# Moving the last output-weight load behind the last V blocks, and giving the wait for the output to GpSimd

## The chip, the cores and the metric

One core of a Trainium2 chip. The metric is the device time of one execution in microseconds, median of several runs. "The trace" is the hardware profile of one of those executions; its span (first to last instruction) is about 1.8 us less than the device time.

## The reference

One decode step of grouped-query attention over a long cache, mixed by a gate with a small MLP. Only the attention matters here:

```python
def _A_ref(x, k_cache, v_cache, wq, wo):         # x [1,1,448], caches [1,8,65536,256] bf16
    q = (x @ wq).reshape(1, 1, 16, 256)...       # 16 query heads, 8 key/value heads, 2 queries share one
    scores = jnp.einsum("bhqd,bhkd->bhqk", q, k) * (256 ** -0.5)
    p = _softmax(scores, axis=-1)
    o = jnp.einsum("bhqk,bhkd->bhqd", p, v)
    return o.transpose(...).reshape(1, 1, 16 * 256) @ wo      # wo [4096, 448]
...
return g * a + (1 - g) * b                       # a: attention, b: MLP, g: gate
```

The two caches are 537 MB. Everything else is small.

## The kernel before

The sequence is cut into 48 chunks (8 key/value heads, 6 chunks each, 5 or 6 times 2048 positions). All large loads are issued by SyncE, in one order that is also the order of the DMA queue. K has two buffers, V one; a load waits until its buffer is free (`s_vf`). The output weights of a head group (512 rows of `wo`, 448 KB) have one buffer, and are loaded once for each group behind the group's second V chunk:

```python
        load_k(2)
        for i in range(1, total - 1):
            load_v(i)
            if i % PER == 1 and i > PER:       # PER = 6 chunks for each head group
                load_wo(i // PER)              # waits for s_oo: the group before has used its weights
            if i + 2 < total:
                load_k(i + 2)
        ...
        vlast = kbuf[(total - 2) % 2]          # the last V chunk goes to a free K buffer, in four pieces
        edges = [0, nlast - TURN - SB, nlast - TURN, nlast - TAIL, nlast]    # rows 0, 40, 56, 76, 80
        for k in range(len(edges) - 1):
            lo, hi = edges[k] * DH, edges[k + 1] * DH
            sp.dma_start(out=vlast[:, lo:hi], in_=src[:, lo:hi]).then_inc(s_last[k], 16)
```

At the end, the last 24 rows of V are used as stationary operand ("turned"), so that the head's output comes out as a column; then the output weights are applied and the row is stored:

```python
        pe.wait_ge(s_last[2], 16)
        turned(edges[2], edges[3])             # 40 matmuls
        pe.wait_ge(s_last[3], 16)
        turned(edges[3], edges[4]).then_inc(s_fp, 1)     # 8 matmuls
        take(dve, s_wo, 16)
        dve.wait_ge(s_fp, 4)
        heads().then_inc(s_fd, 1)              # VectorE: oT = PSUM * gate / denominator
        pe.wait_ge(s_fd, 4)
        for k in range(4):
            cc, r = divmod(k, 2)               # r: which of the two heads
            for a in range(4):
                ins = pe.matmul(acc4[32 * a:32 * a + 1, 0:DQ], lhsT=oT[:, k:k + 1],
                                rhs=wo[:, r, cc, DQ * a:DQ * (a + 1)], ...)
        ins.then_inc(s_fp, 1)
        dve.wait_ge(s_fp, 5)
        dve.tensor_copy(out=res[0:97, :], in_=acc4[0:97, 0:DQ]).then_inc(s_fd, 1)
        sp.wait_ge(s_fd, 5)
        sp.dma_start(out=out[0, 0]..., in_=res[0:97:32, :]).then_inc(s_out, 16)
        sp.wait_ge(s_out, 16)
```

After this the language adds an end: SyncE signals all engines, each drains and answers, SyncE collects the answers, and a barrier in two rounds follows.

The softmax here doesn't subtract the row's maximum and nothing guards it: scores larger than these inputs give would overflow.

## Time and profile before

| | before |
|---|---|
| device time, median of 3 | 1268.15 us (1268.02 to 1268.16) |
| span of the profiled run | 1266.2 us |
| DMA, share of 16 engines' span | 99.5%, 544 MB at 430 GB/s |
| PE, VectorE busy | 57%, 53% |

The page's second part (busy tenths in 40 slices) and its third (queue, packets, MB, share of 16 engines) show a kernel with nothing left but bytes:

```profile
DMA  9999999999999999999999999999999999999997
...
q1 hardware_dynamic: 16728, 544.22, 99.5%
```

So only the two ends of the span can shrink. The chain of waits, in order of time (start, length, what; all in us), ends so:

```profile
1229.60 0.04 issue
1229.64 31.00 DMA kbuf<-in_A_v_cache_dram
1260.64 0.05 issue
1260.69 1.44 PE misc L798 x48
1262.13 0.02 issue
1262.15 0.17 DVE oT L569
1262.33 0.04 issue
1262.37 0.57 PE acc L831 x14
1262.94 0.02 issue
1262.96 0.27 DVE res L838
```

The 31 us are the time a V piece spends in the queue, not the time it takes. What counts is 1260.64: the landing that lets PE start the 48 turned matmuls. The chain stops at `res`; the rest is read from SyncE's waits (who waited for whom: us in total, times, longest):

```profile
SPq L841 <- DVE res L838: 32.7, 1, 32.7
...
SPq L846 <- DMA out_dram<-res: 1.0, 1, 1.0
```

The trace has the store issued at 1263.27, its last semaphore step at 1264.92, and 1.29 us more to the end of the span.

### The profile page before, as it was taken

Reading aid. Unit: us, or ns where it says so; the run is one execution under the profiler, and the core shown is the slowest. Engines: PE = TensorE matmul, PEld = TensorE weight load, DVE = VectorE, ACT = ScalarE, POOL = GpSimd, SP = SyncE. Lnnn points to the kernel's source line nnn. Section 1 sums busy time; section 2 is a strip of 40 time slices with the busy share of each in tenths; the row PEclk is TensorE's granted clock in tenths of the full one; section 3 lists DMA queues with packets and bytes.
Section 4 is the critical chain, followed back from the end, with each engine's and each line's share of the span. In section 5 each row is a group of like instructions: output and inputs, shape, how many; then the busy total and the mean of one; then the engine's idle time right before and its main releaser. Section 6 shows DMA issues by size and latency. Waiting matters only on the chain. (4 is left out here: it accounts for less than half of the span.)

```text
span 1266.2 us, 10795 instructions
## 1 busy us (share of the span) xinstructions
PE 719.7 (57%) x4344; PEld 281.9 (22%) x4344; DVE 665.2 (53%) x473; ACT 50.1 (4%) x127; POOL 76.8 (6%) x98
## 2 busy tenths in 40 slices
PE   2845656566554665456555664565545655467646
PEld 1311222122221222122222221222212222122212
DVE  4745554465544645455445554565445644465444
ACT  0000000000000000000000000000000000000000
POOL 0001010110101101101111011000000000000000
PEclk9887877778777778778877788778867778777787
DMA  9999999999999999999999999999999999999997
GB/s 409 420 442 435 427 439 435 425 435 443 424 437 434 433 438 434 430 429 432 436 439 434 429 435 438 425 438 434 435 433 436 430 430 435 437 436 434 429 432 323
DMA packets 16828, 544.35 MB, mean 430 GB/s; under 512 B 1840, under 2 KB 3890, under 8 KB 4146
## 3 DMA queue, kind: packets, MB, share of 16 engines
q1 hardware_dynamic: 16728, 544.22, 99.5%
q8 instruction: 4, 0.07, 0.0%
q14 instruction: 6, 0.05, 0.0%
q10 hardware_dynamic: 90, 0.01, 0.0%
HBM read 544.22 MB, written 0.00 MB: 430 GB/s over the span
## 5 line engine op out<-in xcount | busy, mean ns | idle before, releaser
L677 PE MATMUL sc<-kT,qw 128*128 128x512 bf16 x2048 | 562.7, 437 | 455.9 <-PEq L673 455.9
L551 DVE STREAM_TRANSPOSE kT<-kbuf 128x2048 f32<-128x2048 f32 x256 | 571.1, 2283 | 309.6 <-DVEq L543 309.6
L677 PEld LDWEIGHTS sc<-kT,qw 128*128 128x128 bf16 x2048 | 213.5, 108 | 804.1 <-issue 639.6
L691 PE MATMUL pv<-vbuf,pT 128*4 128x512 bf16 x2008 | 132.4, 417 | 56.7 <-PEq L725 56.7
L597 DVE STREAM_TRANSPOSE pT<-p_t 128x512 bf16<-128x512 bf16 x48 | 34.1, 711 | 116.9 <-DVEq L543 116.9
L562 DVE TENSOR_TENSOR og<-pv,og 128x512 f32<-128x512 f32 x39 | 27.0, 691 | 111.1 <-DVEq L543 108.5
L691 PEld LDWEIGHTS pv<-vbuf,pT 128*4 128x4 bf16 x2008 | 51.4, 93 | 136.0 <-issue 98.1
L624 ACT ACTIVATE p_t<-sc 128x512 bf16<-128x512 f32 x48 | 28.7, 597 | 1191.8 <-PE sc L677 1191.8
L651 POOL TENSOR_SCALAR t_b<-t_b 128x448 f32<-128x448 f32 x14 | 7.9, 564 | 358.2 <-ACT t_b L633 358.2
L655 POOL TENSOR_SCALAR t_b<-t_b,hw 128x448 f32<-128x448 f32 x14 | 8.9, 638 | 335.4 <-ACT t_b L641 335.4
L561 DVE COPY og<-pv 128x512 f32<-128x512 f32 x8 | 5.5, 691 | 38.9 <-DVEq L543 38.9
L660 POOL TENSOR_TENSOR ymix<-ymix,t_b 128x448 f32<-128x448 f32 x14 | 16.1, 1148 | 1.1
L747 PE MATMUL acc<-wo,oT 128*1 128x448 bf16 x28 | 8.7, 445 | 12.7 <-PEq L744 12.7
L654 POOL TENSOR_TENSOR t_b<-t_b,u_b 128x448 f32<-128x448 f32 x14 | 15.8, 1127 | 1.2
L659 POOL TENSOR_TENSOR t_b<-t_b,u_b 128x448 f32<-128x448 f32 x14 | 15.8, 1126 | 1.2
L633 ACT ACTIVATE t_b<-h_bc,b1T,w1T 128x448 f32<-128x448 f32 x14 | 10.5, 748 | 0.0
L647 POOL TENSOR_SCALAR u_b<-h_bc,w1T,b1T 128x448 f32<-128x448 f32 x14 | 10.0, 714 | 4.1 <-DVE pat L426 2.7
L624 ACT ACTIVATION_READ_ACCUMULATOR p_t<-sc 128x1 f32 x48 | 9.3, 194 | 0.0
L701 PEld LDWEIGHTS misc<-mask,og 128*128 128x128 f32 x64 | 8.7, 196 | 2.3 <-DVE og L562 1.3
L701 PE MATMUL misc<-mask,og 128*128 128x2 f32 (+1 forms) x64 | 8.0, 249 | 0.8 <-DVE og L562 0.8
L641 ACT ACTIVATE t_b<-t_b 128x448 f32<-128x448 f32 x14 | 7.9, 566 | 0.0
L747 PEld LDWEIGHTS acc<-wo,oT 128*1 128x1 bf16 x28 | 2.2, 91 | 15.4 <-issue 14.5
(98 smaller groups left out, 55.6 us busy)
## 6 DMA issues: line engine op xcount, KB each, us to landing
kbuf<-in_A_k_cache_dram SPq DMA_DIRECT2D x32, 5120.0 KB, 33.2
vbuf<-in_A_v_cache_dram SPq DMA_DIRECT2D x31, 5120.0 KB, 20.8
kbuf<-in_A_k_cache_dram SPq DMA_DIRECT2D x16, 6144.0 KB, 36.0
vbuf<-in_A_v_cache_dram SPq DMA_DIRECT2D x16, 6144.0 KB, 24.7
wo<-in_A_wo_dram SPq DMA_DIRECT2D x8, 448.0 KB, 22.1
vbuf<-in_A_wq_dram SPq DMA_DIRECT2D x1, 3072.0 KB, 10.2
kbuf<-in_A_v_cache_dram SPq DMA_DIRECT2D x1, 2560.0 KB, 26.5
kbuf<-in_A_v_cache_dram SPq DMA_DIRECT2D x1, 1280.0 KB, 31.0
```

Of the source, the lines that this page charges most:

```text
L551: dve.transpose(out=kT[b][:].bitcast(FP32), in_=kn[:, s * SB * 128:(s + 1) * SB * 128]).then_inc(s_kt, 1)
L562: return dve.tensor_tensor(out=og[:], in0=pv[:], in1=og[:], op=ALU.add)
L597: dve.transpose(out=pT[:], in_=p_t[:]).then_inc(s_pt, 1)
L624: ins = act.activation(out=p_t[:], in_=sc[:], func=ACT.Exp, scale=scale, accum_out=den[:, c:c + 1])
L633: ins = act.activation(out=t_b[:], in_=h_bc[:], func=ACT.Square, scale=w1T[:, b:b + 1], bias=b1T[:, b:b + 1],)
L654: lambda: pool.tensor_tensor(out=t_b[:], in0=t_b[:], in1=u_b[:], op=ALU.mult),
L659: lambda: pool.tensor_tensor(out=t_b[:], in0=t_b[:], in1=u_b[:], op=ALU.mult),
L660: lambda: pool.tensor_tensor(out=ymix[:], in0=ymix[:], in1=t_b[:], op=ALU.add),
L677: ins = pe.matmul(sc[:], lhsT=qw[:, q, at:at + 128], rhs=kv[:, :, q // 2, :, q % 2], start=(first and q == 0), stop=(last and q == 7), ski ...
L691: ins = pe.matmul(pv[32 * a:32 * a + 4, :], lhsT=pT[:, k, :, ROW0 + s], rhs=vt[:, j * DH:(j + 2) * DH], start=first and k < 4, stop=last a ...
L701: ins = pe.matmul(o_ps[:, cc, 0:width if half == 0 else 2], lhsT=og[:, half * DH + cc:(half + 1) * DH:2], rhs=mask[:, m:m + (width if half ...
L747: ins = pe.matmul(acc[0:1, 0:D], lhsT=oT[:, k:k + 1], rhs=wo[:, r, cc, :], start=False, stop=False, skip_group_check=True,)
```

## The change

The last group's weights are not needed before the very last matmuls. The intent is to let them use the time in which PE and VectorE work on the last V rows, and to bring V forward by the time the weights took in front of it. The second head's weights get their own semaphore, and the loop is turned so that the first head's matmuls come first. The final wait moves to GpSimd, so that SyncE can start the closing exchange while the store is in flight.

```diff
-            if i % PER == 1 and i > PER:
+            if i % PER == 1 and PER < i < total - PER:
                 load_wo(i // PER)
@@ behind the four last V pieces
+        sp.wait_ge(s_oo, HKV - 1)
+        s_wl = [nc.alloc_semaphore(f"s_wl{r}") for r in range(2)]
+        for r in range(2):
+            at = (HKV - 1) * 512 + r * DH
+            sp.dma_start(
+                out=wo[:, r, :, :].rearrange("p c n -> p (c n)"),
+                in_=A_wo[at:at + DH, :].rearrange("(p c) n -> p (c n)", c=2),
+            ).then_inc(s_wl[r], 16)
@@ at the end
-        take(dve, s_wo, 16)
...
-            cc, r = divmod(k, 2)
+            r, cc = divmod(k, 2)
+            if cc == 0:
+                pe.wait_ge(s_wl[r], 16)
...
-                    acc4[32 * a:32 * a + 1, 0:DQ], lhsT=oT[:, k:k + 1],
+                    acc4[32 * a:32 * a + 1, 0:DQ], lhsT=oT[:, 2 * cc + r:2 * cc + r + 1],
...
-        sp.wait_ge(s_out, 16)
+        pool.wait_ge(s_out, 16)
```

No byte is added or taken away. Line numbers of the end of the kernel grow by 8 or 9.

## The prediction

> **What bounds the kernel.** DMA. The page's DMA row is 9 in every slice but the last; the queue table puts the SyncE queue at 99.5% of 16 engines' span, 544 MB at a mean of 430 GB/s. The Trainium skill ("DMA: Bandwidth & Descriptors", Specifications) gives a fabric ceiling of 435 GB/s; the trace agrees: there is nothing left in the body. PE (57%) and DVE (53%) are not limits. Only the tail after the last byte can shrink. In the chain of waits: the last V pieces land (31 us in the queue, until 1260.64), 48 turned-V matmuls 1.44, oT 0.17, 16 output matmuls 0.57, res 0.27, all with small hops; then the trace has the output DMA issued at 1263.27, landing at 1264.92, and barriers until 1266.2.
>
> **What the change does.** No byte is added or removed. The eighth output-weight load (448 KB), which sat between V(43) and K(45), now comes last in the queue, as two of 224 KB. In the trace this load took 1.18 us of each DMA engine (16 packets of 1792 B, 74 ns each; its last semaphore step came 1.18 us after that of V(43), 1174.87 to 1176.05). Everything queued behind it should arrive 1.18 us sooner: the last two V pieces, whose last steps came at 1260.64 and 1261.27, at 1259.46 and 1260.09. The compute between V's landing and the first use of the weights (1.73 us) hides their transfer.
>
> The queue doesn't run dry: the last V pieces were issued at 1229-1230 and landed 31 us later. The SyncE wait for s_oo was met before 1154.
>
> Are the weights there in time? A DMA counts as landed when the slowest engine's step comes (same page, "Why a DMA increments its semaphore by 16"; here first and last step of the last V piece are 2.69 us apart, agreeing that engines finish independently). The slowest engine's total is unchanged, so the second head's weights land near 1261.28, the first's near 1260.69. Output matmuls should start near 1261.19 (1262.37 - 1.18), the ninth near 1261.33 plus a wait of about 0.05. Both are met, the second by only about 0.1 us. That is the tight step.
>
> **The final wait.** Before: landing 1264.92, SyncE wakes 1264.94, branches, signals all engines at 1265.12, they drain and answer by 1265.21, SyncE collects three waits, ending 1265.43. After: SyncE signals while the output is in flight; only GpSimd's answer is late: wake and branch (about 0.17 as on SyncE), drain 0.04, one hop, then SyncE's last wait. Estimate 1265.2 instead of 1265.41: 0.2 us saved.
>
> **Sum.** -1.18 (V sooner) - 0.2 (barrier) + 0.05 (waits on PE) = -1.33 us: **1266.8 us**, range 1266.3 to 1267.4. Faster by over 2%: 1%. Within 2%: 97%. Slower: 2% (a disturbed run only).
>
> **What would show it.** V's last pieces landing about 1.2 us sooner; the turned matmuls starting near 1259.5; output matmuls near 1261.2 with at most 0.1 us idle between the heads; res about 1.1-1.2 us sooner; landing of the output to the end of the span 1.1 us instead of 1.3.
>
> **What would make it wrong.** Small trailing DMAs costing more than their packets, so the second head's weights land after 1261.5 and PE waits for them (gain 0.8-1.0); an instruction fetch landing on the slowest DMA engine (16 KB packets of 0.88 us are in the trace near the end) and delaying it; GpSimd waking or branching more slowly than SyncE, which would cancel the 0.2.

## The result, and the profile after

| | before | after |
|---|---|---|
| device time, median of 4 | 1268.16 us (1268.02 to 1268.33) | 1266.83 us (1266.68 to 1266.91) |
| span of the profiled run | 1266.2 us | 1265.1 us |

The ratio is 0.9989, with a 95% interval of 0.9972 to 1.0007. A ratio is the mean time of one kernel's runs over that of the other's of the same rounds, so not quite the ratio of the medians quoted. The interval contains 1; but the ranges of the runs do not touch, and they did not in after_again, below. The medians differ by 1.33 us. The two profiled runs differ by 1.08 us only, in device time (1267.99 and 1266.91) as in span: the profile of before fell on a run faster than its median, that of after on one of its slowest. Readings of single traces carry that.

The end of the chain of waits, after:

```profile
1228.82 0.04 issue
1228.87 30.97 DMA kbuf<-in_A_v_cache_dram
1259.84 0.05 issue
1259.88 1.42 PE misc L806 x48
1261.30 0.02 issue
1261.32 0.17 DVE oT L577
1261.50 0.04 issue
1261.54 0.57 PE acc L840 x14
1262.11 0.02 issue
1262.14 0.28 DVE res L847
```

It has the same steps with the same lengths (1.42, 0.17, 0.57 and 0.28 us, as before to within 0.02). The whole chain begins 0.80 us sooner, because V landed 0.80 us sooner; the weights, now last in the queue, do not appear in it. PE's wait before the output matmuls is still one for `oT`, and still 0.26 us long (timeline: start, length, instruction; in brackets the idle time before it and what ended it), first before, then after:

```profile
1262.37 0.54 PE L831 MATMUL acc<-wo,oT 128*1 128x112 bf16 x16 [0.26 <-DVE oT L569]
```

```profile
1261.54 0.54 PE L840 MATMUL acc<-wo,oT 128*1 128x112 bf16 x16 [0.26 <-DVE oT L577]
```

SyncE's waits after:

```profile
SPq L850 <- DVE res L847: 31.7, 1, 31.7
...
SPq L855 <- POOLq L855: 0.6, 1, 0.6
```

The wait for the store has turned into one for GpSimd's answer. The trace has the store's last step at 1264.09 and 1.04 us more to the end: 0.24 us less than before. 0.83 us (`res` ends sooner) and 0.24 us, with rounding, are the 1.08 us by which the spans differ.

The closing exchange, from the semaphore events of the two traces (us; "landing" is the store's last step):

| | before | after |
|---|---|---|
| SyncE signals all engines | landing + 0.20 | 0.93 before the landing |
| the waiting engine wakes and branches | SyncE: + 0.05 | GpSimd: + 0.06 |
| GpSimd's drain ends | + 0.27 | + 0.23 |
| SyncE's last wait ends | + 0.51 | + 0.27 |
| end of the span | + 1.29 | + 1.04 |

Before, the signal, every engine's drain and SyncE's three waits all come after the landing; after, only GpSimd's drain and SyncE's last wait do.

### The profile page after: what moved, and what is told of

Its sections match the earlier page's. It is cut to its first block, busy times and chain, and to the rows that moved or that the text cites. A ratio compares the mean times of both kernels' runs of the same rounds, so it can differ in the third digit from the quotient of the medians.

```text
span 1265.1 us, 10796 instructions
## 1 busy us (share of the span) xinstructions
PE 721.0 (57%) x4344; PEld 282.1 (22%) x4344; DVE 665.3 (53%) x473; ACT 50.1 (4%) x127; POOL 77.0 (6%) x98
```

## The experiments

Two theories stood against each other from the start. **Mine**: the two parts add; the load is worth the DMA time of its bytes in front of V, and costs nothing at the end. **Rivals**: the gain is the final wait alone; or it is SyncE's saved issue and wait in mid-stream, which held up the K load behind it; or the weights are still paid for at the end, and V's place is worth more than it seems. In each call the kernel before ran beside the others on the same chip; its medians in the three calls were 1268.09, 1268.10 and 1268.12 us (9 runs each), so differences to it can be compared across calls. Every kernel below has 5 timed runs.

A load raises its semaphore in 16 steps, one for each DMA engine; the trace has the time of each. "V landed" is the last step of the third V piece, which starts the turned matmuls; "the exchange" is the time from the store's landing to the end of the span. Both, and the landing of the weights, are from the kernel's one trace.

### pool_only: the final wait alone

```diff
  # kernel before
-        sp.wait_ge(s_out, 16)
+        pool.wait_ge(s_out, 16)
```

> The kernel before with only the last wait given to GpSimd. If the two parts of the change add up, this one is worth the 0.24 us by which the stretch from the output's landing to the end of the span shrank in the trace (1.29 to 1.04 us): about 1267.9 us where before is 1268.15, with V's last landings where before has them. If the wait is worth nothing by itself, 1268.15. If it is most of the gain, below 1267.3.

Measured: 1267.88 us (1267.73 to 1267.98) against 1268.09 (1267.98 to 1268.14), ratio 0.9998: 0.21 us. V landed at 1260.62 (before: 1260.64); the exchange took 1.04 us (before: 1.29). SyncE now waits for GpSimd's answer instead of the store:

```profile
SPq L846 <- POOLq L846: 0.6, 1, 0.6
```

### move_only: the weights alone

```diff
  # changed kernel
-        pool.wait_ge(s_out, 16)
+        sp.wait_ge(s_out, 16)
```

> The changed kernel with the last wait back on SyncE. If the two parts add up: 1.0 to 1.2 us under before, about 1267.1 us; landing of the output to the end of the span 1.29 us as before. If the move needs the GpSimd wait to pay (SyncE's later issues in its way), near 1268.

Measured: 1267.05 us (1266.93 to 1267.15), ratio 0.9992: 1.04 us under before. V landed at 1259.71; the exchange took 1.29 us, with SyncE's wait for the store back in its place:

```profile
SPq L855 <- DMA out_dram<-res: 1.0, 1, 1.0
```

The parts work apart from each other. Their sum, 1.25 us, is close to the whole: 1.33 us in the first rounds, 1.40 in after_again.

### no_load: the last weights not loaded at all (result wrong)

```diff
  # changed kernel
-        for r in range(2):                      # and the s_oo wait before it
-            sp.dma_start(out=wo[:, r, :, :]...).then_inc(s_wl[r], 16)
...
-            if cc == 0:
-                pe.wait_ge(s_wl[r], 16)
```

> The changed kernel without the last weight load and its waits: it computes with the weights of the group before, so the result is wrong on purpose. If the load is hidden behind the work after V's landing, as the prediction holds, the time stays within 0.15 us of the changed kernel's (1266.8). If the load at the end costs PE a wait, this is faster by that wait, 0.3 us or more. If only V's place in the queue mattered and the load were paid at the end, faster by about 1.2 us.

Measured: 1266.62 us (1266.51 to 1266.70), ratio 0.9988: 0.08 us under after_again and 0.21 under the first rounds of the changed kernel (0.21 is over the 0.15 expected; counted from the kernel before of each call, the two differences are 0.07 and 0.14). In the trace V landed at 1259.54, and from the first turned matmul to the first output matmul it took 1.65 us, as in the changed kernel (1.66). So the load at the end is hidden but for 0.1 to 0.2 us at most. The comparison with the reference still called this result correct: the weights of the wrong group stay within its tolerance, which is worth knowing for anyone who moves a load here: a correct output does not show that these weights came in time.

### again_mid: the same bytes once more at the old place

```diff
  # changed kernel; junk is a tile that nothing reads
             if i % PER == 1 and PER < i < total - PER:
                 load_wo(i // PER)
+            if i == total - PER + 1:
+                sp.dma_start(out=junk[:], in_=A_wo[(HKV - 1) * 512:HKV * 512, :]...).then_inc(s_junk, 16)
```

> The changed kernel with the same 448 KB loaded a second time, at the old place in the queue, into a tile that nothing reads. If the gain is the engine time of those bytes ahead of V, the turned matmuls start 1.18 us later than in the changed kernel and the time rises by 1.0 to 1.2 us, to about 1268.0. If the gain came from the weights' new place itself or from the two smaller loads, the time stays near 1266.8.

Measured: 1267.99 us (1267.92 to 1268.16), 1.29 us over after_again. V landed at 1260.87, 1.30 us later than in after_again and 1.03 later than in the first trace of the changed kernel; the mean of its 16 steps came 1.15 us later than in after_again. The start of the turned matmuls, first in after_again, then in again_mid:

```profile
1259.62 1.40 PE L806 MATMUL misc<-pT,kbuf 128*128 128x2 bf16 x48 [0.57 <-DMA kbuf<-in_A_v_cache_dram]
```

```profile
1260.92 1.44 PE L813 MATMUL misc<-pT,kbuf 128*128 128x2 bf16 x48
```

The bytes in front of V are what the move removes. The old wait for `s_oo` is not in this run, so it is not needed to explain the time.

### tiny_mid: the issue at the old place, without the bytes

```diff
+            if i == total - PER + 1:
+                sp.dma_start(out=junk[:, 0:1, 0:2], in_=A_wo[0:128, 0:2]...).then_inc(s_junk, 16)
```

> The changed kernel with a load of 4 bytes for each partition at the old place: SyncE's issue of 0.43 us is there again, the bytes are not. If bytes are what matters, at most 0.15 us over the changed kernel (8 small packets on each engine). If it was the issue, and the wait before it, that held up the K load behind it, about 0.5 us over it or more.

Measured: 1266.89 us (1266.68 to 1266.93), 0.19 us over after_again (1266.63 to 1266.75; the ranges overlap). V landed 0.08 us later. That is a little over the 0.15 expected and far from 0.5: SyncE's issue in mid-stream, with K loads waiting some 30 us in the queue anyway, is not the cause.

### after_again: the changed kernel

> The changed kernel once more, unchanged, so that the others of this call have it on the same chip: 1266.8 us, 1.25 to 1.35 us under before. If the two parts measured apart (0.21 and 1.04 us) add, 1.25. In the trace the turned matmuls should start 0.8 to 1.2 us before those of the kernel before (1260.69)[...].

Measured: 1266.70 us (1266.63 to 1266.75) against 1268.10, ratio 0.9989: 1.40 us. V landed at 1259.58, 1.07 us before that of before, and the second head's weights at 1261.32. In both traces of this kernel the output matmuls came in four groups of four, 0.05, 0.09 and 0.09 us apart, exactly as before, so the second head's weights cost the matmuls nothing. But it was as tight as can be: PE's weight load for the second head came 0.087 us after that for the first (before: 0.051), in both traces 0.042 us after the landing (1261.583 to 1261.625 in the first). The semaphore held it for some 0.035 us, which the matmuls before it covered.

### one_load: the last weights as one load

```diff
-        s_wl = [...]; for r in range(2): ... one load for each head
+        sp.dma_start(out=wo[:].rearrange("p r c n -> p r (c n)"), in_=A_wo[(HKV - 1) * 512:HKV * 512, :]...).then_inc(s_wl, 16)
...
-            if cc == 0:
-                pe.wait_ge(s_wl[r], 16)
+            if k == 0:
+                pe.wait_ge(s_wl, 16)
```

> The changed kernel with the last weights as one load of 448 KB and one wait before the first output matmul. If the second head's weights land just when they are needed (in the trace 1261.58 for a use at 1261.63), the one load holds the first head's matmuls to that time too: they start 0.1 us later at most, and the time rises by 0.0 to 0.1 us. If splitting by head carries a good part of the gain, 0.3 us or more.

Measured: 1266.99 us (1266.84 to 1267.09), 0.29 us over after_again, no overlap. I had sized this too small. The timeline shows the wait:

```profile
1259.73 1.40 PE L804 MATMUL misc<-pT,kbuf 128*128 128x2 bf16 x48 [0.57 <-DMA kbuf<-in_A_v_cache_dram]
1261.16 0.16 DVE L575 TENSOR_TENSOR oT<-misc,rden 128x4 bf16<-128x4 f32 x1 [3.16 <-PE misc L804]
1261.55 0.31 PEld L838 LDWEIGHTS acc<-wo,oT 128*1 128x1 bf16 x16 [0.51 <-DVE oT L575]
1261.58 0.54 PE L838 MATMUL acc<-wo,oT 128*1 128x112 bf16 x16 [0.45 <-DMA wo<-in_A_wo_dram]
```

PE's idle time before the output matmuls is 0.45 us instead of 0.26 in the changed kernel, and it ends with the weights, not with `oT`. They landed at 1261.44; the first matmul came 0.14 us later; why it took that long is not shown (in the changed kernel it starts 0.05 us after `oT` is ready). So the split by head is worth 0.2 (trace) to 0.3 us (times): at most a fifth of the gain.

### finer: V's last pieces made smaller

```diff
-        edges = [0, nlast - TURN - SB, nlast - TURN, nlast - TAIL, nlast]
+        edges = [0, nlast - TURN - SB, nlast - TURN, nlast - 12, nlast - TAIL, nlast]   # and one wait more on PE
```

> The changed kernel with the 20 V rows of the third late piece loaded as 12 and 8, so that their turned matmuls start before the last V bytes are there. In the trace of the changed kernel V's last step came at 1260.20 to 1260.47 and the turned matmuls end 0.8 us later, so V's side alone could give about 0.4 us. But if the second head's weights, which land at 1261.32 to 1261.58, come next, PE must wait for them, the two heads' output matmuls are drawn apart by about 0.4 us, and the time falls by only 0.0 to 0.1 us. If the weights are not next, by 0.3 us or more.

Measured: 1266.69 us (1266.56 to 1266.75), 1.43 us under before; the changed kernel had 1.40. In its timeline:

```profile
1260.32 0.29 PEld L806 LDWEIGHTS misc<-pT,kbuf 128*128 128x128 bf16 x8 [0.15 <-DMA kbuf<-in_A_v_cache_dram]
1260.74 0.16 DVE L577 TENSOR_TENSOR oT<-misc,rden 128x4 bf16<-128x4 f32 x1 [2.79 <-PE misc L806]
1260.95 0.12 PEld L842 LDWEIGHTS acc<-wo,oT 128*1 128x1 bf16 x8 [0.34 <-DVE oT L577]
1260.98 0.82 PE L842 MATMUL acc<-wo,oT 128*1 128x112 bf16 x16 [0.28 <-DVE oT L577]
1261.44 0.10 PEld L842 LDWEIGHTS acc<-wo,oT 128*1 128x1 bf16 x8 [0.36 <-DMA wo<-in_A_wo_dram]
```

`oT` is ready at 1260.90 instead of 1261.22 to 1261.49, and PE's weight loads then idle 0.36 us for the second head's weights. The 0.4 us gained on V's side turned into a new wait; 0.03 us were left.

### finer2: and the second head's weights in two loads

```diff
  # finer; three loads: (r=0, both halves), (r=1, first half), (r=1, second half)
-            if cc == 0:
-                pe.wait_ge(s_wl[r], 16)
+            if k != 1:
+                pe.wait_ge(s_wl[max(0, k - 1)], 16)
```

> As the run before it, and the second head's weights in two loads of 112 KB, so that only 4 matmuls are left when the last bytes land. If the end of the DMA queue with the little work behind it is the limit, 0.1 to 0.2 us under the changed kernel, about 1266.6 us. If the shorter rows (896 B) or the one more load cost the DMA engines time, no gain.

Measured: 1266.63 us (1266.51 to 1266.75), 1.49 us under before, 0.09 better than the changed kernel's 1.40. The gain has the right sign and about the expected size, but it is within the scatter of runs; it is the best version found, and not shown to be better.

### probe15: a V piece kept off one DMA engine

In the first trace of the changed kernel one DMA engine lands the last loads 2.9 us after the first and 1.1 us after the next-latest. By the rule of the Trainium skill ("DMA: Bandwidth & Descriptors", "Why a DMA increments its semaphore by 16 and not by 1"), a transfer uses the largest number of engines up to 16 that divides its slowest dimensions, the lowest-numbered ones: 120 partitions would leave the sixteenth engine free.

```diff
-            sp.dma_start(out=vlast[:, lo:hi], in_=src[:, lo:hi]).then_inc(s_last[k], 16)
+            if k == 1:                     # 120 partitions, then 8, on one semaphore; PE waits for 32
+                sp.dma_start(out=vlast[0:120, lo:hi], in_=src[0:120, lo:hi]).then_inc(s_last[k], 16)
+                sp.dma_start(out=vlast[120:128, lo:hi], in_=src[120:128, lo:hi]).then_inc(s_last[k], 16)
+                continue
```

> The changed kernel with the second of the last four V pieces loaded as 120 partitions and then 8, so that by the Trainium skill's rule for how many DMA engines a transfer uses one engine (the highest-numbered) carries none of it and saves 8 packets of 309 ns, 2.47 us, while eight others carry one packet more. The trace has one engine landing 2.9 us after the first, 1.1 us after the second-latest. If that late engine is the highest-numbered, the last landing comes 1.0 us sooner and the time falls by about 0.7 to 1.0 us, to 1265.9. If it is another one, the last landing comes where it did or 0.3 us later (1266.8 to 1267.1), and an engine lands 2.5 us ahead of the rest.

Measured: 1272.51 us (1272.21 to 1272.74), ratio 1.0035: 5.7 us slower than the changed kernel, which neither theory of the run had foreseen. Stretches of the trace (start:end, length, busy time of PE, PEld, DVE, ACT and POOL with counts in brackets, granted clock, DMA share, GB/s), first the changed kernel:

```profile
1240.00:1250.00 10.00, 9.13 (x34) 3.52 (x33) 7.55 (x4) 0.00 (x0) 0.00 (x0) 0.81 0.95 412
1250.00:1260.00 10.00, 7.81 (x98) 3.42 (x97) 2.68 (x7) 0.69 (x2) 0.00 (x0) 1.00 0.90 371
```

and this one:

```profile
1240.00:1250.00 10.00, 9.13 (x41) 3.61 (x43) 7.20 (x4) 0.05 (x1) 0.00 (x0) 0.92 0.97 420
1250.00:1260.00 10.00, 6.11 (x72) 1.76 (x64) 1.99 (x6) 0.64 (x2) 0.00 (x0) 0.76 0.99 252
```

The engines were busy 99% of the second stretch but moved 252 GB/s. Packets of 8192 bytes, which are those of the split piece, ran at a median of 12 to 18 GB/s in each microsecond from 1252 on instead of 26.5, and those of the pieces queued before and behind were slowed too. The split itself did what the rule says: the semaphore of the two loads has 2 events at their issue and then 23 at landings, the sum of the 15 and 8 engines that the rule gives for 120 and 8 partitions. One engine did land 1.5 to 2.0 us ahead of the second in the loads behind it, so some engine carried less; whether the late engine was the one spared can't be read under that slowdown. Why the split halves the rate is open.

## Why the prediction was right

- **The sum**: 1266.8 predicted, 1266.83 measured in the first rounds. That it fits to 0.03 us is in part luck: runs of one kernel scatter by more, V's term was 0.14 us too large by move_only, the 0.05 us on PE did not appear, and the same kernel gained 1.40 us in after_again. The mechanism is what the runs below show.
- **The final wait**: predicted 0.2 us; the exchange shrank from 1.29 to 1.04 us in every trace that has the change (pool_only, the changed kernel, again_mid and others) and in none without it (before, move_only); 0.21 us in the times of pool_only. Shown.
- **V sooner**: predicted 1.18 us, from the load's time on each engine. The times give 1.04 (move_only against before) to 1.29 us (again_mid against after_again), and again_mid and tiny_mid show that it is the bytes. In the traces V landed 0.80, 1.07 and 0.93 us sooner (changed kernel twice, move_only), so this term was sized somewhat too large for the traces at hand. The mean of the 16 steps shifted more evenly, by 1.03, 1.06 and 1.12 us. What differs is how far the last DMA engine lags behind the first: 2.69 us before, 2.99, 2.64 and 2.87 us in those three (at the last V piece). After the first 60 us the lag grows by more than 0.3 us only once in each trace (probe15's slowed end aside), at the V load that lands near 1200 us: by 0.64 us before, by 0.79 to 0.99 us in the changed kernel and its variants but 0.60 in probe15. An instruction fetch of 8 KB, 0.31 us long, is recorded at 1197 to 1198 us in every trace, and the 40 KB packet that starts just as it ends took 2.05 to 2.07 us in each, where others took 1.51. So the fetch delayed one engine, by some 0.85 us as an estimate from these figures (0.31 and 0.55). That it was the last engine is argued, because the traces do not name a packet's engine, and whether the changed kernel draws a larger jump by its nature is open: again_mid, with the weights' bytes back in their place, had 0.97, pool_only 0.68.
- **The weights in time**: predicted to land at 1261.28 with about 0.1 us to spare, and a wait of 0.05 us on PE. They landed at 1261.58 and 1261.32, 0.30 and 0.04 us later than that, as V too came 0.38 and 0.12 us later than its 1259.46. Of the 0.1 us to spare nothing was left: PE's weight load for the second head was held some 0.035 us by them, but the four groups of output matmuls lie as far apart as before. The term of 0.05 us did not appear in the sum. Calling this the tight step was right: one_load lost 0.2 to 0.3 us there, and in finer it became the next limit.
- **The queue does not run dry**, and SyncE's wait for `s_oo` cost nothing: the two weight loads were issued at 1229.8 and 1230.3, 31 us before they landed.

The terms measured apart, 1.04 and 0.21 us, make 1.25 where 1.33 was predicted and 1.33 and 1.40 were measured; the remainder of about 0.1 us is within the scatter of the runs.

## What to carry to other kernels

In a kernel that is bound by one DMA queue, what counts is not only how many bytes there are but which come last: put last what has the least work behind it, and let it land under the work of what came before; a load that is not needed until then costs about its whole DMA time if it stands in front (here 1.0 to 1.3 us for 1.18). After such a move the load itself can be next in line (here nothing was left to spare), so give its first part its own semaphore and use it first. At the very end, let another engine wait for the store than the one that starts the closing exchange (here 0.2 us).

## What the Trainium skill lacked or had wrong

- "DMA: Bandwidth & Descriptors", Specifications: its fabric ceiling of 435 GB/s agrees with the 430 GB/s over the whole span. Its row of 358 GB/s for HBM per core was exceeded by a fifth in this program of one core; the row leaves out what "Perfetto Trace Analysis", Roofline, says: that this is a core's share when both of a pair are active, and that a single core can pull more.
- "DMA: Bandwidth & Descriptors", "Why a DMA increments its semaphore by 16 and not by 1": the engines do finish independently, 2.6 to 3.0 us apart at the end of these traces (probe15 aside). The page does not say that the distance stays: in the trace of before it was 0.9 us after the first load, 2.3 us by 43 us, and later loads took less than 0.2 us of it back before it rose again.
- The same section tells how many engines a partition count gets, but not what an uneven split costs: one V piece as 120 and 8 partitions brought its packets in the following 9 us from 26.5 down to 12 to 18 GB/s and cost 5.7 us. No other page has this case.
- "Runtime: NRT & Kernel Launch", "Instruction fetch mechanics", calls the crossing of a block mostly hidden. Here fetches take time of the DMA engines that carry the data: their packets of 16 KB took 0.88 to 0.97 us in the trace of before and those of 8 KB 0.31 us, and at 1198 us the data packet that followed one took 2.07 us instead of 1.51. The last engine's lag grew from 0.86 to 1.94 us at the load during which the first of these fell (25.9 us), so in a kernel bound by DMA they may well show at the end; no run here tested it.
- No page has the cost of waiting for the last store on the engine that starts the closing exchange: 0.24 us, the difference between the traces with that wait (1.29 us) and those without (1.04).
